# A Fourier layer with a top-k MoE on one core: the first stage as one 98 by 98 product, and DRAM scratch laid out for all partitions

## The chip, the cores and the metric

The kernel runs on one core of a Trainium2 chip. The metric is the time of one execution on the device in microseconds (us); lower is better. PE is TensorE, ACT is ScalarE, DVE is VectorE, POOL is GpSimd, SP is SyncE, which here only starts DMAs.

## The reference, cut to what matters

The input x is 8 x 3136 x 256 fp32. A real FFT over the 3136 rows of a batch, a complex 256 x 256 product with bias, a soft threshold and the inverse FFT give y. A gate then scores every row of y; the 128 best rows of each batch get the result of a two-layer network added, weighted by the sigmoid of their score.

```python
X = np.fft.rfft(x, axis=1)                     # 8 x 1569 x 256
Yr = Xr @ w_r - Xi @ w_i + b_r
Yi = Xr @ w_i + Xi @ w_r + b_i
Yr = np.sign(Yr) * np.maximum(np.abs(Yr) - 0.01, 0.0)   # Yi alike
y = np.fft.irfft(Yr + 1j * Yi, n=3136, axis=1)
scores = y @ w_gate
top_idx = np.argpartition(-scores[b], 128)[:128]        # per batch
xe = y[b, top_idx]
ye = np.maximum(xe @ w1, 0.0) @ w2
out[b, top_idx] = xe + sigmoid(scores[b, top_idx])[:, None] * ye
```

## The kernel before, in words

The 3136 rows are seen as 98 x 32, and both transforms are done in two steps by matrix products, with scratch arrays in DRAM between the steps because the steps need different axes on the partitions.

- `ld_x` loads x, one tile (`xt`) for two calls of the first step, into partitions 0..48 and 64..112: rows a and a + 49 of the 98 side by side. `fold` (L391) makes their sum and difference (`sd`), two instructions per call, on POOL; for batch 0 mostly on DVE.
- `s1` (L402) multiplies `sd` by cosines and sines: four fp32 products of 49 x 49 with 512 columns, one on each 64 x 64 quadrant of the array. ACT copies the result to `at` (L404), and a store puts it into the scratch `As`. There are 8 calls per batch.
- `ld_a` loads `av` from `As`, one tile for two groups; `s2` (L448) does the second step in 32 small fp32 products on quadrants. ACT writes the rounded half `Xh` (L454), DVE the rest `Xl` (L455). There are 13 groups per batch, 104 in all, one for each iteration of the main loop.
- `spectral` (L222 to L224) makes the complex product in 18 fp32r matmuls. ACT copies a part out (`ks`, L469), POOL adds the bias (`kb`, L471), DVE adds the two (`py`, L475). `shrink` does the threshold with ACT (`r`, L480) and DVE (`Y`, L482).
- `s2i` (L500) is the first step back; ACT copies it to `ct` (L507), DVE takes the scores on the way (`junk`, `Csc`, L509), and a store puts `ct` into the scratch `Cs`. `ld_c` loads `cv` from there, `s1i` (L547) is the last step, ACT copies to `ot` (L549), and `ov` stores go to the output.
- `route`, `select` and `place` find the best rows with many small DVE instructions (L239, L243, L265 among them) and small products on PE (L250) that share the PSUM tile `pca` with `s2i`. `fetch` and `ffn` (L325 to L372) gather them, run the network (L353 its first product) and scatter the rows.

The order is written out by hand in the loop `for t in range(-1, B * G + 20)`. An iteration flushes the stores of the one before it on SP, issues loads on SP, and then runs s2 of group t+1, one call of s1 or s1i, spectral of group t, s2i of group t-1, shrink of group t, and a second call of s1 or s1i if one is due. s1 works 17 groups ahead of s2 (`LEAD`), s1i 18 behind (`LAG`). `av` has two buffers and is asked for two iterations before its use.

DMAs are started on SP's queue or on ACT's. `move` (L151) puts the second half of x, As, av, cv and output transfers on a list, and `issue_late` (L157 to L159) issues that list on ACT's queue, in an iteration right behind the spectral product: behind `ks`, ahead of `ct`.

```python
def move(odd, out, src):
    if odd:
        late.append((out, src))
    else:
        nc.sync.dma_start(out=out, in_=src)
...
    py, r = spectral(*divmod(t, G), lambda: turn("db"))
...
issue_late()
for b, i in steady(t + LEAD + 2):
    fold(b, i, nc.gpsimd)
...
s2i(*divmod(t - 1, G))
```

Of the kernel before, what the change touches and what calls it, by code (L numbers as in the profile page):

```python
# [27 lines left out]
def _tables():  # L28
    m = np.arange(NH)
    n2 = np.arange(N2)  # L30
    n4 = np.arange(64)
    w = np.zeros((2, 64, 3, 64))
    we, wi = w[0, :NH, :2], w[0, :NH, 2]
    g = np.zeros((2, 2, N2, NJ - 1, 3, N2))
    gi = np.zeros((2, 2, N2, NP, 2, 2, 64))
    for j in range(NJ - 1):
        e = 2 * j + 2
        for p, r in enumerate((e, NH - e if e < NH else 0)):
            a = 2 * np.pi * ((m * r) % N1) / N1
# [20 lines left out]
    we[:, 0, NH - 1] = 1.0  # L60
    we[:, 1, NH - 1] = 1.0 - 2.0 * (m % 2)
    wi[NH - 1, :NH] = 1.0
    w[1] = w[0]
    gt = np.zeros((2, N2, 3, NF))
    gti = np.zeros((NF, 2, 64))
    slots = [(0, 98 * k2) for k2 in range(17)] + [(1, 49 + 98 * k2) for k2 in range(16)]
    for s, (q, k) in enumerate(slots):
        a = 2 * np.pi * ((n2 * k) % S) / S
        edge = k in (0, S // 2)
        gt[q, :, 0, s] = np.cos(a)  # L70
        gt[q, :, 1, s] = -np.sin(a)
# [8 lines left out]
    return (w.reshape(128, 3, 64), g.reshape(128, NJ - 1, 3 * N2), gi.reshape(128, NP, 2, 128),  # L80
            gt.reshape(NF, 3, NF), gti, wq.reshape(NJ, 4, N1))
# [19 lines left out]
def fourier_moe(ctx: ExitStack, tc: tile.TileContext, x, w_r, w_i, b_r, b_i, wg, w1, w2,  # L101
                t_w, t_wq, t_g, t_gi, t_gt, t_gti, t_m, t_dig, outs, cap):
# [10 lines left out]
    xv = x.rearrange("b (h m c) d -> b m h c d", h=2, c=N2)  # L113
    ov = [o.rearrange("(a r c i) d -> c a r (i d)", r=16, c=2, i=2) for o in outs]
    As, Cs, xt, sd, at, ct, av, cv, ot, X, Y, Csc = [{} for _ in range(12)]
    pca, pcb = [ps.tile([128, 2 * D], F32, name=n, bufs=1) for n in ("pca", "pcb")]

# [3 lines left out]
    w = c_tile([128, 3, 64], F32, "w")  # L121
    nc.scalar.dma_start(out=w, in_=t_w)
    xts, cvs = [[c_tile([128, 8, D], F32, n + str(k)) for k in range(2)] for n in ("xt", "cv")]
    for k, t in enumerate(xts + cvs):
        (nc.vector if k % 2 else nc.gpsimd).memset(t[32:64], 0.0)
# [251 lines left out]
    def ld_x(b, i):  # L377
        if i % 2:
            return
        k = i // 2  # L380
        t = xt[b, k] = (cvs if b == 0 and k > 1 else xts)[k % 2].rearrange("p (h c) d -> p h c d", h=2)
        for r in (1, 0):
            move(r, t[64 * r:64 * r + 48], xv[b, :48, :, 8 * k + 4 * r:8 * k + 4 * r + 4, :])
        ld(t[48:113:64], xv[b, 48, :, 8 * k:8 * k + 8, :].rearrange("h (r c) d -> r h c d", r=2))

    def fold(b, i, eng):
        e = i % 2
        t = xt[b, i // 2][:, :, 2 * e:2 * e + 2, :]
        f = sd[b, i] = pool.tile([128, 2, 2, D], F32, name="sd", bufs=2)
        for k, op in enumerate((ALU.add, ALU.subtract)):  # L390
            eng.tensor_tensor(out=f[:113, k], in0=t[:113, 0], in1=t[:113, 1], op=op)  # L391

    def s1(b, i):
        if i == 0:
            As[b] = dram.tile([2, NH, N2, D], F32, name="As")
        if i % 2 == 0:
            at[b] = pool.tile([128, 2, 2, 2 * D], F32, name="ot" if b == 0 and i > 3 else "at", bufs=2)
        f = sd.pop((b, i))
        p = ps.tile([128, 2, 2 * D], F32, name="px" if b == 0 and i % 2 else "s", bufs=1)
        for r in range(2):  # L400
            for c in range(2):
                nc.tensor.matmul(p[64 * c:64 * c + 64, r, :], w[64 * r:64 * r + NH, c, :], f[64 * r:64 * r + NH, c], start=True, stop=True)  # L402
        t = at[b]
        nc.scalar.copy(out=t[:, :, i % 2, :], in_=p)  # L404
        if i % 2 == 0:
            return

        def store():
            n = slice(4 * i - 4, 4 * i + 4)
            for q in range(2):  # L410
                move(q, As[b][q, :48, n, :], t[64 * q:64 * q + 48])
            nc.sync.dma_start(out=As[b][:, 48, n, :], in_=t[48:113:64])
# [251 lines left out]
    issue_late()  # L664
    consts_g(1)
    first = {i + 1: i for i in range(U)}
    fold(1, 0, nc.gpsimd)
    fold(1, 1, nc.gpsimd)
    rest = [(b, i) for b in range(B) for i in range(U)]
    for t in range(-1, B * G + 20):  # L670
# [3 lines left out]
        if t + 4 in first and first[t + 4] > 3:  # L674
# [41 lines left out]
        for b, i in steady(t + LEAD + 2):  # L716
            fold(b, i, nc.gpsimd)
        if t + 2 in first and first[t + 2] > 1:
            fold(1, first[t + 2], nc.gpsimd)
# [40 lines left out]
```

## Time and profile before

| what | value |
|---|---|
| three runs | 854.99, 855.54 (median), 863.56 us |
| the profiled execution | 854.73 us, its span 853.0 us |
| PE busy (matmuls) | 703.0 us, 82% of the span |
| DVE, ACT, POOL busy | 516.5, 368.8, 304.6 us |
| TensorE clock granted, mean of the span | 0.902 of full |
| DMA | 163.74 MB in 87757 packets, mean 192 GB/s |

Busy is the time in which an engine's instructions run; overlapping matmuls are counted once. [...] "DMA share" is the mean busy share of the 16 DMA engines. In a row, "x8" is a count of records (one fp32 matmul leaves two), and "[2.04 <-DVE Csc L509]" says that the engine sat idle for 2.04 us before it, until Csc was written by line 509. ACTq and SPq are the instruction queues of ACT and SP, where a DMA issue stands.

### The profile page before, as it was taken

To read this page: it belongs to the slowest core of one execution; us is meant where nothing else is said; L and a number is where in the kernel's file an instruction comes from. 1 tells how busy PE (TensorE), PEld (TensorE's weight loads), DVE (VectorE), ACT (ScalarE), POOL (GpSimd) and SP (SyncE) were. 2 spreads that over 40 slices of the span, in tenths; PEclk is the share of its full clock that TensorE was granted. 3 is DMA by queue.
4 is the path that set the end of the run, shared out by engine and by line. 5 is a ranking of instruction groups with operands and counts; after the bars stand their busy time and mean duration, and the time that the engine had idled before them with its cause. 6 is when DMAs were issued, how large, how long until landed. Compare 5 with 4: busy or idle time off the path is not lost. (4 is left out here: it accounts for less than half of the span.)

```text
span 853.0 us, 20524 instructions
## 1 busy us (share of the span) xinstructions
PE 703.0 (82%) x8220; PEld 517.0 (61%) x8220; DVE 516.5 (61%) x1339; ACT 368.8 (43%) x667; POOL 304.6 (36%) x264
## 2 busy tenths in 40 slices
PE   2749899988788978888898889888889888778876
PEld 0337667665565656565676667666667677645465
DVE  3415456544377867765457757676457989971640
ACT  1315455545354544354354434455455444532200
POOL 2126574444354524444334424346341311220000
PEclk9859999999899998898899989899899999995679
DMA  9878998999889897889798877889877748659600
GB/s 164 227 188 176 234 232 187 238 266 263 198 232 228 215 219 181 208 218 224 158 234 228 202 169 167 216 202 238 196 197 194 191 106 172 172 131 215 154 25 13
DMA packets 87757, 163.74 MB, mean 192 GB/s; under 512 B 7697, under 2 KB 61038, under 8 KB 81390
## 3 DMA queue, kind: packets, MB, share of 16 engines
q1 hardware_dynamic: 59230, 97.23, 45.6%
q10 hardware_dynamic: 27536, 63.02, 32.6%
q0 software_dynamic: 896, 2.17, 0.9%
q8 instruction: 65, 1.06, 0.6%
q14 instruction: 30, 0.25, 0.1%
HBM read 84.35 MB, written 78.12 MB: 190 GB/s over the span
## 5 line engine op out<-in xcount | busy, mean ns | idle before, releaser
L471 POOL TENSOR_TENSOR kb<-ks,bias 128x512 f32<-128x512 f32 (+1 forms) x104 | 133.9, 1287 | 414.9 <-ACT ks L469 403.1
L391 POOL TENSOR_TENSOR sd<-xt 113x512 f32<-113x512 f32 x114 | 143.4, 1279 | 33.0 <-DMA xt<-in_x 18.9
L475 DVE TENSOR_TENSOR py<-py,kb 128x512 f32<-128x512 f32 (+1 forms) x104 | 72.3, 695 | 108.1 <-POOL kb L471 79.8
L507 ACT COPY ct<-pcb 128x256 f32<-128x256 f32 x96 | 35.7, 371 | 228.8 <-PE pcb L500 173.8
L455 DVE TENSOR_TENSOR Xl<-px,Xh 128x768 fp32r<-128x768 f32 x96 | 91.9, 957 | 58.5 <-ACT Xh L454 58.2
L448 PE MATMUL px<-g_sb,av 64*64 64x96 f32 x3072 | 90.5, 250 | 35.7 <-DMA av<-As 33.6
L448 PEld LDWEIGHTS px<-g_sb,av 64*64 64x64 f32 x3072 | 81.4, 136 | 60.3 <-DMA av<-As 25.2
L500 PE MATMUL pca<-Y,gi_sb 64*64 64x256 f32 x768 | 108.6, 403 | 0.0
L500 PE MATMUL pcb<-Y,gi_sb 64*64 64x256 f32 x768 | 108.5, 403 | 0.0
L454 ACT CAST Xh<-px 128x768 fp32r<-128x768 f32 x96 | 77.2, 805 | 41.7 <-PE px L448 23.5
L402 PE MATMUL s<-sd,w 49*64 49x512 f32 x480 | 74.1, 646 | 20.3 <-DVE sd L391 15.4
L547 PE MATMUL s<-cv,w 49*64 49x512 f32 x464 | 73.6, 660 | 17.2 <-ACT ot L549 16.8
L480 ACT ACTIVATE r<-py,m2l 128x512 f32<-128x512 f32 (+1 forms) x104 | 72.4, 696 | 31.6 <-DVE py L475 31.4
L509 DVE CUSTOM_DVE_ANT_0 junk<-pcb,wgb 128x256 f32<-128x256 f32 x96 | 40.4, 421 | 62.5 <-ACT ct L507 61.7
L222 PE MATMUL pcb<-wsh,Xh 128*128 128x256 f32 x208 | 72.6, 349 | 1.5 <-DVE Csc L509 1.5
L482 DVE SCALAR_TENSOR_TENSOR Y<-py,r 128x512 f32<-128x512 f32 (+1 forms) x104 | 71.2, 685 | 2.9 <-ACT r L480 2.9
L222 PEld LDWEIGHTS pcb<-wsh,Xh 128*128 128x128 f32 x208 | 42.7, 205 | 45.9 <-issue 28.3
L404 ACT COPY at<-s 128x1024 f32<-128x1024 f32 x58 | 59.9, 1033 | 21.9 <-PE s L402 21.4
L549 ACT COPY ot<-s 128x1024 f32<-128x1024 f32 x58 | 59.2, 1021 | 19.6 <-PE s L547 18.0
L500 PEld LDWEIGHTS pca<-Y,gi_sb 64*64 64x64 f32 x768 | 47.5, 139 | 29.3 <-issue 6.1
L222 PE MATMUL py<-wnh,Xh 128*128 128x256 f32 x208 | 62.8, 302 | 1.3 <-DVE Y L482 1.2
L222 PE MATMUL py<-wdh,Xh 128*128 128x256 f32 x208 | 62.9, 303 | 0.0
(133 smaller groups left out, 1503.6 us busy)
## 6 DMA issues: line engine op xcount, KB each, us to landing
Cs<-ct SPq DMA_DIRECT2D x48, 512.0 KB
av<-As ACTq DMA_DIRECT2D x48, 256.0 KB
av<-As SPq DMA_DIRECT2D x48, 256.0 KB
xt<-in_x ACTq DMA_DIRECT2D x30, 384.0 KB
xt<-in_x SPq DMA_DIRECT2D x30, 384.0 KB
As<-at ACTq DMA_DIRECT2D x30, 384.0 KB
As<-at SPq DMA_DIRECT2D x30, 384.0 KB
cv<-Cs SPq DMA_DIRECT2D x30, 384.0 KB
```

Source lines behind the costliest of these rows:

```text
L222: nc.tensor.matmul(out, wh, mh, start=start, stop=False)
L391: eng.tensor_tensor(out=f[:113, k], in0=t[:113, 0], in1=t[:113, 1], op=op)
L402: nc.tensor.matmul(p[64 * c:64 * c + 64, r, :], w[64 * r:64 * r + NH, c, :], f[64 * r:64 * r + NH, c], start=True, stop=True)
L448: nc.tensor.matmul(o[:, :, N2 * j:N2 * j + N2], a[64 * p:64 * p + 64, 2 * (g % 2) + j, 128 * h + 64 * q:128 * h + 64 * q + 64], g_sb[64 * ...
L454: nc.scalar.copy(out=vh, in_=v)
L455: nc.vector.tensor_tensor(out=vl, in0=v, in1=vh.bitcast(F32), op=ALU.subtract)
L471: nc.gpsimd.tensor_tensor(out=kb[:r], in0=ks[:r].broadcast_to([r, 2, D]), in1=bias[:r], op=ALU.add)
L475: nc.vector.tensor_tensor(out=py[:r], in0=py[:r], in1=kb[:r], op=ALU.add)
L480: nc.scalar.activation(out=r1[:r], in_=py[:r], func=AF.Relu, bias=m2l[:r], scale=1.0)
L482: nc.vector.scalar_tensor_tensor(out=y[:r], in0=py[:r], scalar=0.0, in1=r1[:r], op0=ALU.min, op1=ALU.add)
L500: nc.tensor.matmul(p[q][64 * a:64 * a + 64], gi_sb[64 * q:64 * q + 64, g, c, 64 * a:64 * a + 64], y[64 * q:64 * q + 64, c, :], start=(c == ...
L547: nc.tensor.matmul(p[64 * c:64 * c + 64, r, :], w[64 * r:64 * r + NH, 2, :], f[64 * r:64 * r + NH, 4 * e + 2 * c:4 * e + 2 * c + 2, :], st ...
```

## The change

The first step is one 98 x 98 product per 512 columns, on x as it lies in DRAM. `fold` and its tiles are gone. `xt` holds one of the 98 rows on each of 98 partitions, and there are three such buffers instead of two. `As` is 98 x 32 x 256. `Cs` is 2 x 64 x 32 x 256 in three fixed DRAM tiles with 15 rows of padding per half, which `pads` fills with zeros once, at t = 3. `Cs` stores come in two, one for even and one for odd rows; `cv` loads span 128 partitions. Output runs are 4 KB. Columns of `gi` and `gti` are permuted to match. `warm`, which runs matmuls on constants, stands at the very start and gets a POOL memset and four DVE transposes. At the start, batch 1 gets three x tiles ahead instead of two, and every second s1 copy of batch 0 is on DVE. x, As, av and cv are no longer split over `move`.

```diff
     def ld_x(b, i):
-        t = xt[b, k] = (cvs if b == 0 and k > 1 else xts)[k % 2].rearrange("p (h c) d -> p h c d", h=2)
-        for r in (1, 0):
-            move(r, t[64 * r:64 * r + 48], xv[b, :48, :, 8 * k + 4 * r:8 * k + 4 * r + 4, :])
-        ld(t[48:113:64], xv[b, 48, :, 8 * k:8 * k + 8, :].rearrange("h (r c) d -> r h c d", r=2))
+        t = xt[b, k] = (xts[:2] + cvs)[k] if b == 0 else xts[(4 * b + k + 1) % 3]
+        ld(t[:96], xv[b, :96, 8 * k:8 * k + 8, :])
+        ld(t[96:N1], xv[b, 96:, 8 * k:8 * k + 8, :])
-    def fold(b, i, eng):
-        e = i % 2
-        t = xt[b, i // 2][:, :, 2 * e:2 * e + 2, :]
-        f = sd[b, i] = pool.tile([128, 2, 2, D], F32, name="sd", bufs=2)
-        for k, op in enumerate((ALU.add, ALU.subtract)):
-            eng.tensor_tensor(out=f[:113, k], in0=t[:113, 0], in1=t[:113, 1], op=op)
     def s1(b, i):
-        for r in range(2):
-            for c in range(2):
-                nc.tensor.matmul(p[64 * c:64 * c + 64, r, :], w[64 * r:64 * r + NH, c, :], f[64 * r:64 * r + NH, c], start=True, stop=True)
+        for h in range(2):
+            n = 4 * (i % 2) + 2 * h
+            nc.tensor.matmul(p[:N1, h, :], w, f[:N1, n:n + 2, :], start=True, stop=True)
-        nc.scalar.copy(out=t[:, :, i % 2, :], in_=p)
+        if b == 0 and i % 2:
+            nc.vector.tensor_copy(t[:N1, i % 2], p[:N1])
+        else:
+            nc.scalar.copy(out=t[:N1, i % 2], in_=p[:N1])
...
-            for q in range(2):
-                move(q, As[b][q, :48, n, :], t[64 * q:64 * q + 48])
-            nc.sync.dma_start(out=As[b][:, 48, n, :], in_=t[48:113:64])
+            nc.sync.dma_start(out=As[b][:96, n, :], in_=t[:96])
+            nc.sync.dma_start(out=As[b][96:, n, :], in_=t[96:N1])
     def ld_a(b, g):
...
-            for q in range(2):
-                move(q, av[b, g][64 * q:64 * q + 64], As[b][q, :48].rearrange("(j c) n d -> (c n) j d", c=2)[:, 2 * g:2 * g + 4])
+            ld(av[b, g], As[b][:96].rearrange("(j c) n d -> (c n) j d", c=4)[:, 2 * g:2 * g + 4])
     def s2i(b, g):
...
-            stores.append(lambda: nc.sync.dma_start(out=Cs[b][:48].rearrange("(j q) n d -> (q n) j d", q=2)[:, 2 * g - 2:2 * g + 2], in_=t))
+            def store():
+                for q in range(2):
+                    nc.sync.dma_start(out=Cs[b][q, :48].rearrange("(j a) n d -> (a n) j d", a=2)[:, 2 * g - 2:2 * g + 2], in_=t[q::2])
+            stores.append(store)
+    def pads():
+        z = pool.tile([128, 2, 2, 2 * D], F32, name="ot", bufs=2).rearrange("p r s (o x) -> p o (r s x)", o=1)
+        nc.gpsimd.memset(z, 0.0)
+        for t in Csd:
+            for q in range(2):
+                ld(t[q, NH:].rearrange("m n d -> m (n d)").rearrange("m (k x) -> m k x", k=4), z[:64 - NH].broadcast_to([64 - NH, 4, 2048]))
     def ld_c(b, i):
-        for r in range(2):
-            move(r, t[64 * r:64 * r + 48], Cs[b][:48, 16 * k + 8 * r:16 * k + 8 * r + 8, :])
-        ld(t[48:113:64], Cs[b][48, 16 * k:16 * k + 16].rearrange("(r n) d -> r n d", r=2))
+        ld(t, Cs[b].rearrange("r m n d -> (r m) n d")[:, 8 * k:8 * k + 8, :])
     def s1i(b, i):
...
             for c in range(2):
-                move(c, ov[b][c, :48, n, :], t[64 * c:64 * c + 48].rearrange("p r s x -> p (r s) x"))
+                move(c, ov[b][c, :48, i // 2], t[64 * c:64 * c + 48].rearrange("p r s x -> p r (s x)"))
...
+    warm()
     for i in range(U):
         ld_x(0, i)
-    issue_late()
...
         if i == 4:
             ld_x(1, 0)
             ld_x(1, 2)
+            ld_x(1, 4)
         flush()
-        issue_late()
     weights()
-    warm()
```

On ACT, in iteration t = 40 (batch 3, group 1), the order of before is this; `DMA` rows are issues on ACT's queue, the rest are its own copies.

```order
L469 COPY ks<-pcb 128x256
L159 DMA As<-at 48x2048
L159 DMA out<-ot 48x4x512
L159 DMA xt_73<-in_x 48x2x1024
L159 DMA av<-As 64x4x256
L507 COPY ct<-pcb 128x256
L507 COPY ct<-pca 128x256
L480 ACTIVATE r_3593<-py,m2l 128x512
L454 CAST Xh<-px 128x2x12x32
L404 COPY at<-s 128x2x512
```

The changed kernel has this there.

```order
L467 COPY ks<-pcb 128x256
L165 DMA out<-ot 96x1x1024
L505 COPY ct<-pcb 128x256
L505 COPY ct<-pca 128x256
L478 ACTIVATE r_3365<-py,m2l 128x512
L452 CAST Xh<-px 128x2x12x32
L405 COPY at<-s 98x1024
```

Three of the four DMA issues between `ks` and `ct` have left ACT; only the half of the output store is still there.

On SP, in the iterations t = 40 to t = 42 (there is nothing for it to issue in t = 41), from the output store on, before has this; every row is a DMA issue.

```order
L155 DMA out<-ot 48x4x512
L557 DMA out<-ot 2x4x512
L155 DMA xt_73<-in_x 48x2x1024
L149 DMA xt_73<-in_x 2x2x1024
L155 DMA av<-As 64x4x256
L515 DMA Cs<-ct 128x4x256
L155 DMA av<-As 64x4x256
L155 DMA cv_74<-Cs 48x2048
L149 DMA cv_74<-Cs 2x2048
```

The changed kernel:

```order
L161 DMA out<-ot 96x1x1024
L565 DMA out<-ot 2x2x1024
L155 DMA xt_78<-in_x 96x2048
L155 DMA xt_78<-in_x 2x2048
L155 DMA av<-As 128x4x256
L518 DMA Cs_72<-ct 64x4x256 x2
L155 DMA av<-As 128x4x256
L155 DMA cv_80<-Cs_71 128x2048
```

What was split over both queues stands whole on SP's, in the same order; the `av` load behind a `Cs` store is now the whole tile, not half of it.

## Rows read from the trace of the kernel before

**Rows 1.** windows by stage: us, busy us (xrecords), PEclk, DMA share, GB/s
```profile
0.00:52.00 52.00, 21.53 (x78) 8.78 (x78) 17.95 (x25) 9.90 (x10) 13.64 (x14) 0.86 0.83 192
52.00:660.00 608.00, 527.67 (x6688) 393.02 (x6692) 374.49 (x908) 295.95 (x540) 258.66 (x220) 0.92 0.87 211
660.00:767.00 107.00, 88.33 (x1153) 70.23 (x1142) 95.53 (x274) 47.35 (x96) 25.37 (x23) 0.97 0.65 156
```

**Rows 2.** waits of PE, 52 to 660 us: us in total, times, longest
```profile
PE px L448 <- DMA av<-As: 33.6, 19, 10.2
PE s L547 <- ACT ot L549: 16.8, 8, 3.4
PE pca L250 <- DVE Csc L509: 15.8, 8, 2.7
```

**Rows 3.** timeline of ACT around iteration t = 40: start, us, instruction
```profile
311.28 0.37 ACT L469 COPY ks<-pcb 128x256 f32<-128x256 f32 x1 [0.29 <-PE pcb L224]
...
312.20 2.27 ACTq L159 DMA_DIRECT2D xt<-in_x  x1
314.51 2.28 ACTq L159 DMA_DIRECT2D av<-As  x1
316.89 0.37 ACT L507 COPY ct<-pcb 128x256 f32<-128x256 f32 x1 [5.24 <-DMA out<-ot]
```

**Rows 4.** timeline of PE, two stretches
```profile
315.30 1.03 PE L402 MATMUL s<-sd,w 49*64 49x512 f32 x8
318.36 0.17 PE L250 MATMUL pca<-n,tm 98*98 98x6 bf16 x1 [2.04 <-DVE Csc L509]
...
333.38 0.17 PE L250 MATMUL pca<-n,tm 98*98 98x6 bf16 x1 [2.67 <-DVE Csc L509]
```

**Rows 5.** ACT's av issues by source line L159: ns min/median/max, first and last start
```profile
L159 ACTq DMA_DIRECT2D av<-As x48: 580/592/2737, 43.1 to 728.4; - x48
```

**Rows 6.** timeline of POOL, 325 to 334 us
```profile
327.49 1.27 POOL L471 TENSOR_TENSOR kb<-ks,bias 128x512 f32<-128x512 f32 x1 [3.00 <-ACT ks L469]
328.73 2.49 POOL L391 TENSOR_TENSOR sd<-xt 113x512 f32<-113x512 f32 x2
```

**Rows 7.** timeline of DVE, 328 to 337 us, the same instruction twice
```profile
330.06 1.38 DVE L243 TENSOR_TENSOR c<-scores,f 98x192 bf16<-98x192 f32 x1
...
336.69 0.36 DVE L243 TENSOR_TENSOR c<-scores,f 98x192 bf16<-98x192 f32 x1
```

**Rows 8.** windows of POOL, L391 (the folds) alone, 52 to 660 us
```profile
52.00:660.00 608.00, 136.02 (x108) 0.92 0.87 211
```

**Rows 9.** windows, two short stretches, all engines
```profile
324.10:334.20 10.10, 7.41 (x127) 5.46 (x120) 9.04 (x19) 5.44 (x11) 4.12 (x4) 1.00 0.91 212
334.40:337.60 3.20, 3.20 (x20) 2.74 (x23) 3.03 (x8) 0.68 (x2) 1.28 (x1) 0.50 0.86 182
```

**Rows 10.** windows at the start, columns as in rows 1
```profile
4.00:9.00 5.00, 0.00 (x0) 0.00 (x0) 1.14 (x1) 0.38 (x1) 0.29 (x1) 1.00 1.02 156
9.00:15.00 6.00, 0.00 (x0) 0.00 (x0) 0.32 (x1) 0.00 (x0) 0.00 (x0) 1.00 1.04 218
...
50.00:52.00 2.00, 0.00 (x0) 0.00 (x0) 0.00 (x0) 0.00 (x0) 0.00 (x0) 0.50 1.01 267
```

**Rows 11.** timeline of DVE at the first fold
```profile
14.68 1.90 DVE L391 TENSOR_TENSOR sd<-xt 113x512 f32<-113x512 f32 x3 [9.54 <-DMA xt<-in_x]
```

**Rows 12.** timeline of PE at the first s2
```profile
52.23 1.56 PE L448 MATMUL px<-g_sb,av 64*64 64x96 f32 x32 [10.16 <-DMA av<-As]
```

**Rows 13.** windows of PE, L402 (s1) alone, 52 to 660 us
```profile
52.00:660.00 608.00, 63.08 (x448) 15.60 (x448) 0.92 0.87 211
```

**Rows 14.** records of s1 by source line: ns min/median/max, first and last start
```profile
L402 PE MATMUL s<-sd,w x480: 587/591/1113, 15.4 to 641.8; 49*64 49x512 f32 x160
```

**Rows 15.** timeline of PE at the FFN's first product, full array, fp32
```profile
838.82 2.05 PE L353 MATMUL m<-xT,w1s 128*128 128x128 f32 x16 [0.52 <-DVE xT L338]
```

**Rows 16.** waits of SP's queue, 52 to 660 us
```profile
SPq L515 <- ACT ct L507: 108.0, 31, 8.6
```

More of the change, by code (lines that the diff above doesn't have):

```diff
@@ L31, in _tables @@
     n4 = np.arange(64)
-    w = np.zeros((2, 64, 3, 64))
-    we, wi = w[0, :NH, :2], w[0, :NH, 2]
+    n1 = np.arange(N1)
+    o4 = 2 * (n4 % 32) + n4 // 32
+    wf = np.zeros((N1, NJ - 1, 2, 2))
+    wl = np.zeros((N1, 2))
+    wi = np.zeros((64, 64))
     g = np.zeros((2, 2, N2, NJ - 1, 3, N2))
@@ L72, in _tables @@
         a = 2 * np.pi * ((n4 * k) % S) / S
-        gti[s, 0] = (1.0 if edge else 2.0) * np.cos(a) / S
-        gti[s, 1] = (0.0 if edge else -2.0) * np.sin(a) / S
+        gti[s, 0, o4] = (1.0 if edge else 2.0) * np.cos(a) / S
+        gti[s, 1, o4] = (0.0 if edge else -2.0) * np.sin(a) / S
     gt[:, :, 2] = gt[:, :, 0] + gt[:, :, 1]
@@ L111, in fourier_moe @@
     dram = ctx.enter_context(tc.tile_pool(name="scratch", bufs=3, space=bass.MemoryType.DRAM))
-    xv = x.rearrange("b (h m c) d -> b m h c d", h=2, c=N2)
-    ov = [o.rearrange("(a r c i) d -> c a r (i d)", r=16, c=2, i=2) for o in outs]
-    As, Cs, xt, sd, at, ct, av, cv, ot, X, Y, Csc = [{} for _ in range(12)]
+    xv = x.rearrange("b (a c) d -> b a c d", c=N2)
+    ov = [o.rearrange("(a r k c e i) d -> c a k r (e i d)", r=2, k=4, c=2, e=2, i=2) for o in outs]
+    As, Cs, xt, at, ct, av, cv, ot, X, Y, Csc = [{} for _ in range(11)]
     pca, pcb = [ps.tile([128, 2 * D], F32, name=n, bufs=1) for n in ("pca", "pcb")]
+    Csd = [dram.tile([2, 64, N2, D], F32, name="Cs" + str(k), bufs=1) for k in range(3)]
     def c_tile(shape, dt, name):
         return const.tile(shape, dt, name=name)
-    w = c_tile([128, 3, 64], F32, "w")
+    w = c_tile([N1, N1], F32, "w")
     nc.scalar.dma_start(out=w, in_=t_w)
-    xts, cvs = [[c_tile([128, 8, D], F32, n + str(k)) for k in range(2)] for n in ("xt", "cv")]
-    for k, t in enumerate(xts + cvs):
-        (nc.vector if k % 2 else nc.gpsimd).memset(t[32:64], 0.0)
+    wi_sb = c_tile([128, NF], F32, "wi_sb")
+    nc.scalar.dma_start(out=wi_sb, in_=t_wi)
+    xts = [c_tile([128, 8, D], F32, "xt" + str(k)) for k in range(3)]
+    cvs = [c_tile([128, 8, D], F32, "cv" + str(k)) for k in range(2)]
     g_sb = c_tile([128, NJ - 1, 3 * N2], F32, "g_sb")
@@ L417, in ld_a @@
             av[b, g] = pool.tile([64, 1, D], F32, name="av", bufs=2)
-            for q in range(2):
-                ld(av[b, g][N2 * q:N2 * q + N2, 0, :], As[b][q, 48])
+            ld(av[b, g][:, 0, :], As[b][96:].rearrange("c n d -> (c n) d"))
         elif g % 2 == 0:
             av[b, g] = av[b, g + 1] = pool.tile([128, 4, D], F32, name="av", bufs=2)
-            for q in range(2):
-                move(q, av[b, g][64 * q:64 * q + 64], As[b][q, :48].rearrange("(j c) n d -> (c n) j d", c=2)[:, 2 * g:2 * g + 4])
+            ld(av[b, g], As[b][:96].rearrange("(j c) n d -> (c n) j d", c=4)[:, 2 * g:2 * g + 4])
     def s2(b, g):
@@ L487, in s2i @@
         if g == 0:
-            Cs[b] = dram.tile([NH, 64, D], F32, name="Cs")
+            Cs[b] = Csd[b % 3]
             Csc[b] = pool.tile([128, NJ], F32, name="Csc")
@@ L512, in s2i, with store @@
         if w == 1:
-            stores.append(lambda: nc.sync.dma_start(out=Cs[b][48], in_=t[:r, o, :]))
+            def store():
+                for q in range(2):
+                    nc.sync.dma_start(out=Cs[b][q, 48], in_=t[q:64:2, o, :])
+            stores.append(store)
         elif g % 2 == 1:
-            stores.append(lambda: nc.sync.dma_start(out=Cs[b][:48].rearrange("(j q) n d -> (q n) j d", q=2)[:, 2 * g - 2:2 * g + 2], in_=t))
+            def store():
+                for q in range(2):
+                    nc.sync.dma_start(out=Cs[b][q, :48].rearrange("(j a) n d -> (a n) j d", a=2)[:, 2 * g - 2:2 * g + 2], in_=t[q::2])
+            stores.append(store)
     def score(b):
@@ L525, in score @@
         for q in range(4):
-            nc.tensor.matmul(p, wq[:, q, :], t[:, N2 * q:N2 * q + N2], start=(q == 0), stop=(q == 3))
+            nc.tensor.matmul(p, wq[:, q, :], t[:, 64 * (q // 2) + q % 2:64 * (q // 2) + 64:2], start=(q == 0), stop=(q == 3))
         yield "da"
         nc.vector.tensor_copy(scores[:, b, :], p)
+    def pads():
+        z = pool.tile([128, 2, 2, 2 * D], F32, name="ot", bufs=2).rearrange("p r s (o x) -> p o (r s x)", o=1)
+        nc.gpsimd.memset(z, 0.0)
+        for t in Csd:
+            for q in range(2):
+                ld(t[q, NH:].rearrange("m n d -> m (n d)").rearrange("m (k x) -> m k x", k=4), z[:64 - NH].broadcast_to([64 - NH, 4, 2048]))
     def ld_c(b, i):
@@ L546, in s1i @@
             for c in range(2):
-                nc.tensor.matmul(p[64 * c:64 * c + 64, r, :], w[64 * r:64 * r + NH, 2, :], f[64 * r:64 * r + NH, 4 * e + 2 * c:4 * e + 2 * c + 2, :], start=True, stop=True)
+                nc.tensor.matmul(p[64 * c:64 * c + 64, r, :], wi_sb[64 * r:64 * r + NH], f[64 * r:64 * r + NH, 4 * c + 2 * e:4 * c + 2 * e + 2, :], start=True, stop=True)
         t = ot[b]
@@ L567, in warm @@
             nc.tensor.matmul(p[:, i % 2], pr[:, :128], pr[:, :512], start=True, stop=True)
+        a = pool.tile([128, 2, 2, 2 * D], F32, name="ot", bufs=2).rearrange("p a b c -> p (a b c)")
+        nc.gpsimd.memset(a, 0.0)
+        v = a.rearrange("p (n d) -> p d n", d=64)[:, :16]
+        nc.vector.transpose(out=v, in_=v)
+        nc.vector.transpose(out=a[:, :512], in_=a[:, :512])
+        nc.vector.transpose(out=v, in_=p[:, 0].rearrange("p (n d) -> p d n", d=16))
+        nc.vector.transpose(out=a[:, :512], in_=p[:, 1])
     YB, XB, KB, RB = 2, 2, 1, 1
@@ L653, in fourier_moe @@
     for i in range(U):
-        fold(0, i, nc.gpsimd if i % 3 == 2 else nc.vector)
         s1(0, i)
@@ L673, in fourier_moe @@
             ld_x(b, i)
-        if t + 4 in first and first[t + 4] > 3:
+        if t + 4 in first and first[t + 4] > 5:
             ld_x(1, first[t + 4])
@@ L689, in fourier_moe @@
             consts_gi((t + 1) // 2 + 1)
+        if t == 3:
+            pads()
         if t == 8:
@@ L715, in fourier_moe @@
         issue_late()
[L716 to L719, printed above, removed]
         tick(ffns)
```

38 lines of the change are left out of this document (17 added, 21 removed).

## The prediction

> **What bounds the kernel now.** I read the windows by stage first: before the first s2 (0 to 52 us), the main stretch up to the last s1 (52 to 660), the rest of the main loop without x and s1 (660 to 767). What lies behind 767 is routing, FFN and last stores, which the change does not touch. In the main stretch PE is busy 527.7 of 608 us; DVE has 374, ACT 296, POOL 259 [rows 1]. So PE bounds it, with 80.3 us of gaps, and a mean granted clock of 0.92, which costs (1 - 0.92) x 608 = 49 us. Together 129 us lie beside PE's work at full clock. From 660 to 767 DVE is busy 95.5 of 107 us and bounds; no edit takes anything from DVE's work there, so this stretch and the tail count as 0.
>
> Next, who ends PE's gaps. The list of waits names av loads first (33.6 us, of which 10.2 is the one at the start), then copies of ACT and the scores of DVE [rows 2]. An engine in such a list is only the last link, so I went back along two gaps.
>
> The first: PE waits 2.04 us at 318.36 for `Csc`, DVE's reading of what s2i left [rows 4]. DVE reads it behind `ct`, and `ct` starts late: on ACT, between `ks` at 311.28 and `ct` at 316.89, stand DMA issues, two of 2.3 us each, and ACT does nothing else in that time [rows 3]. An av issue on ACT takes 0.59 us in the median but up to 2.7 [rows 5].
>
> The second: PE waits 2.67 us at 333.38, again for `Csc` [rows 4]. Here DVE itself is late. Its instruction of L243 takes 1.38 us while POOL runs `kb` and two folds (327.49 to 331.2), and 0.36 us at 336.69 with POOL's folds out of the way [rows 6, 7]. Folds are 136 of POOL's 259 us [rows 8, 1]; `kb` stays.
>
> [...]
>
> **The change, part by part.**
>
> *The s1 product (cost).* A call is now eight records on quadrants, four at a time: one of 0.59 us [rows 14], all in 1.03 us [rows 4], so the second round starts 0.44 us behind the first. Two full-array fp32 products leave four records, one behind the other: 0.59 + 3 x 0.44 = 1.91 us, 0.88 more. A check from the full array: 16 records of 128 columns take 2.05 us [rows 15], as many columns as four of 512, so 0.8 to 1.0 more. Between 52 and 660 us lie 448 / 8 = 56 calls [rows 13]: **+49 us** (45 to 57), all on the bounding engine. The eight calls of the start wait for x and cost nothing.
>
> *The start (gain).* Up to 9 us only one half of x comes, into 48 partitions: all DMA engines are busy (1.02) but move 156 GB/s; with both halves 218, with loads over 128 partitions 267 [rows 10]. The first fold waits 9.54 us for x, the first s2 10.16 us for av, at 52.23 [rows 11, 12]. By then 52 x 192 GB/s = 10.0 MB have moved [rows 1]; the third x tile of batch 1 adds 98 x 8 KB = 0.8 MB. 10.8 MB at 267 GB/s take 40 us: **-12 us**. At 218 it is 49.5 (-3); without the third tile in the way 37.5 (-15).
>
> [...] The rows of 218 and 267 GB/s, which differ with both halves in flight, are why I stay with 12.
>
> *Gaps of PE (gain).* av: 33.6 - 10.2 = 23.4 us. What makes these loads late is ACT's queue (their second half stands behind `ks` and other issues) and slow x loads ahead of them in the same engines; both go, and I take 18 of 23.4. The other 80.3 - 23.4 = 57 us come from folds, from ACT's issues and from causes that stay (`kb`, output issues, dependences). I take the folds' share of POOL's time, 136 / 259 = 0.53: 30. Together **-48 us**. Bounds: a third of everything, or 85 in 100.
>
> *Clock (gain).* If 48 of 80.3 us of gaps go, 0.6 of the 49 us goes too: **-29 us**.
>
> *Padding, longer loads.* `pads` writes 6 x 15 rows of 32 KB = 2.95 MB, 14 us of DMA time at 211 GB/s, once, beside a loop in which DMA is busy 0.87 [rows 1]: between 0 and 14 us, I take **+2**, since PE has two av buffers to live on. The 128-partition cv loads read 128 instead of 98 rows, 32 x 30 x 8 KB = 8 MB in all, 29 us of DMA time at 267 GB/s. Against it, x's 25.7 MB at 267 instead of about 187 (midway of 156 and 218) save 41 us of it: 0. If that cover fails, it shows as av waits, priced below.
>
> *SP's queue (a risk).* Issues that left ACT stand in SP's queue, which is in order. There a `Cs` store waits for `ct`, 108 us in 31 waits, up to 8.6 each [rows 16], and the av issue stands behind it; before, ACT's half of av went around it. av is asked for two iterations ahead (608 us for 88 iterations, 6.9 each, so 13.8), a mean wait is 3.5: I take 0.
>
> *At nothing:* three x buffers, odd copies of batch 0 on DVE, `warm` and its transposes (DVE and PE are idle up to the first x), 4 KB output runs, permuted tables.
>
> **Sum**, against the profiled execution (854.73; it stands 0.8 under the median, which I leave out): 854.7 - 12 + 49 - 48 - 29 + 2 = **817 us**. A measurement tells 1% from no change: 847 to 864 is "the same".
>
> **The rivals.**
>
> *Nearly all gaps go.* For it: both gaps followed back lead to things that are removed. Against: `kb` stays, routing still waits on DVE. 85 in 100 of 129 is 110, the start -15: 854.7 - 15 + 49 - 110 + 2 = 781 us.
>
> *x loads don't get faster:* not the partitions but the short runs and their distance in DRAM make 156 GB/s. For it: runs are 4 KB now, and no load of x into 98 partitions stands in the trace. Against: one half alone is slower than both. Then the start gains 3, av 8, the other gaps 30, the clock 38 / 80.3 x 49 = 23: 854.7 - 3 + 49 - 38 - 23 + 2 = 842 us.
>
> *Dependences keep the gaps.* Only a third of the 129 us (43) comes back, because PE, ACT and DVE wait for each other in a ring once the issues are gone: 854.7 - 12 + 49 - 43 + 2 = 851 us, no change to tell. For it: ACT's copies and `Csc` are the last links in rows 2.
>
> *SP becomes the bound of av (slower).* Its place is the av issue behind a `Cs` store. If av comes 1 us too late for each of the 44 pairs of iterations of the main stretch, 44 us of gaps arise and 0.6 x 44 = 27 of half clock: 817 + 44 + 27 = 888 us. It is slower than before from (855 - 817) / (1.6 x 44) = 0.54 us per pair on. For it: the 8.6 us wait. Against: 3.5 in the mean of 13.8.
>
> **How the numbers follow.** Forecast 817: 0.52. Nearly all gaps 781: 0.16. x loads as slow 842: 0.11. A third 851: 0.09. SP 888: 0.12. Faster by over 1%: 0.52 + 0.16 + 0.11 = 0.79; same 0.09; slower 0.12. The range leaves out the SP case (0.12) and half of the 781 case (0.08), and takes in 851: 776 to 852 us.
>
> **What would show it.** In the profile after: the first s2 near 40 us, DMA above 218 GB/s while x comes; s1's records near 0.5 us, four in 1.9, PE busier by 49 us in the main stretch less what the clock gives back; no folds, DVE's L243 at 0.36 except beside `kb`; `ct` less than 1 us behind the end of s2i; PE's waits for av under 10 us; PEclk near 0.97 in the main stretch. It is wrong if PE's gaps stay at 60 us or more there, if av leads the waits again, or if the first s2 stays near 50 us.

## The result, and the profile after

The changed kernel takes 827.6 us (median; 824.05 to 832.16) against 855.6: a ratio of 0.9655, 95% interval 0.9576 to 0.9734. Faster by 3 to 4%, inside the range, 11 us above the forecast of 817. The profiled execution is the slowest of the four, 832.16 us, span 830.4.

The windows by stage of the changed kernel: before the first s2, up to the last s1, the rest of the loop (columns as in rows 1).

```profile
0.00:43.00 43.00, 19.30 (x46) 9.09 (x46) 13.88 (x19) 5.95 (x6) 2.01 (x5) 0.83 0.87 247
43.00:623.00 580.00, 523.27 (x6288) 379.70 (x6291) 329.40 (x883) 291.65 (x528) 124.05 (x111) 0.96 0.78 230
623.00:727.00 104.00, 89.93 (x1198) 73.67 (x1194) 92.52 (x247) 46.49 (x92) 24.21 (x21) 0.96 0.55 171
```

Against [rows 1] the start is 9 us shorter, and POOL has lost half its work. The middle rows do not hold the same work: the one of before runs 18 us past the last s1 record, this one 4. Cut at the first s2 and at the last s1, before and then after, they are these.

```profile
52.23:641.80 589.57, 509.50 (x6472) 378.76 (x6472) 360.00 (x875) 286.88 (x524) 254.83 (x217) 0.91 0.88 212
43.23:618.80 575.57, 519.07 (x6249) 376.01 (x6249) 327.26 (x878) 289.77 (x525) 122.77 (x110) 0.96 0.78 230
```

So the main stretch is 14 us shorter, and PE's gaps (span less PE busy) went from 80.1 to 56.5 us. The list of PE's waits, over the whole span, does not look repaired:

```profile
PE px L446 <- DMA av<-As: 41.6, 9, 25.8
PE px L446 <- issue: 19.8, 1, 19.8
PE pca L256 <- DVE Csc L507: 9.5, 8, 1.7
PE s L556 <- ACT ot L558: 6.9, 11, 0.7
```

The waits for Csc and ot have shrunk [rows 2], while av is worse, for one wait of 25.8 us. It is in PE's timeline here:

```profile
112.41 1.56 PE L446 MATMUL px<-g_sb,av 64*64 64x96 f32 x32 [25.75 <-DMA av<-As]
```

And this is what SP's queue did ahead of it:

```profile
67.08 0.39 SPq L155 DMA_DIRECT2D av<-As  x1
67.52 0.50 SPq L155 DMA_DIRECT2D gi_sb<-t_gi  x1
68.12 19.53 SPq L155 DMA_DIRECT2D Cs<-ot  x6
87.70 4.89 SPq L155 DMA_DIRECT2D g_sb<-t_g  x1
92.70 4.56 SPq L411 DMA_DIRECT2D As<-at  x1
97.30 3.12 SPq L412 DMA_DIRECT2D As<-at  x1
100.52 3.08 SPq L518 DMA_DIRECT2D Cs<-ct  x2
103.69 0.96 SPq L155 DMA_DIRECT2D xt<-in_x  x2
104.69 0.39 SPq L155 DMA_DIRECT2D av<-As  x1
```

`Cs<-ot` x6 are the zero blocks. Their issue takes 19.53 us, the three behind them 3 to 5 each, and the next av is asked for 37.6 us after the last. The windows of that time show what the DMA engines did meanwhile:

```profile
60.00:75.00 15.00, 15.00 (x176) 11.18 (x178) 7.47 (x17) 7.92 (x15) 5.58 (x4) 1.00 0.80 228
75.00:86.00 11.00, 11.00 (x140) 8.04 (x136) 5.99 (x14) 6.52 (x12) 2.19 (x2) 1.00 0.93 111
86.00:100.00 14.00, 0.66 (x15) 0.15 (x4) 2.16 (x6) 1.23 (x3) 0.37 (x1) 0.64 0.85 107
100.00:113.00 13.00, 0.59 (x16) 0.62 (x20) 0.00 (x0) 0.00 (x0) 0.00 (x0) 0.50 0.91 283
```

From 75 to 100 us the DMA engines are 0.85 to 0.93 busy and move only 107 to 111 GB/s, while the zeros leave the 15 partitions that hold them. Without the blocks the DMA engines, as busy (0.94), move 276 GB/s in the stretch that has 111 here (e1, below).

The start: x now comes into 96 partitions at 236 to 246 GB/s [rows 10].

```profile
2.00:6.00 4.00, 2.13 (x5) 1.75 (x6) 1.92 (x2) 1.81 (x2) 0.55 (x1) 1.00 0.98 243
6.00:9.00 3.00, 3.00 (x10) 2.32 (x10) 0.00 (x0) 0.00 (x0) 0.00 (x0) 1.00 1.02 246
9.00:14.00 5.00, 4.73 (x12) 1.72 (x11) 2.59 (x3) 1.01 (x1) 0.00 (x0) 1.00 1.03 236
```

What comes late there is av. On SP's queue its issue follows the last store of batch 0 into As by 10 us:

```profile
29.47 0.23 SPq L412 DMA_DIRECT2D As<-ot  x1
39.29 0.38 SPq L155 DMA_DIRECT2D av<-As  x1
```

On ACT, iteration t = 40 [rows 3] now has one issue, and `ct` waits for PE, not for ACT:

```profile
318.05 0.37 ACT L467 COPY ks<-pcb 128x256 f32<-128x256 f32 x1
318.13 0.58 ACTq L165 DMA_DIRECT2D out<-ot  x1
320.47 0.37 ACT L505 COPY ct<-pcb 128x256 f32<-128x256 f32 x1 [2.05 <-PE pcb L498]
```

An s1 call leaves four records in 1.96 us instead of eight in 1.03 [rows 4]:

```profile
321.00 1.96 PE L400 MATMUL s<-xt,w 98*98 98x512 f32 x4
```

To compare the same work, the next rows run from the `ks` copy of group 12 to that of group 80. First before, then after:

```profile
129.30:609.20 479.90, 412.42 (x5150) 305.39 (x5149) 303.45 (x743) 232.61 (x423) 197.65 (x165) 0.91 0.88 213
```

The changed kernel, the same groups:

```profile
147.60:582.80 435.20, 410.20 (x4982) 295.67 (x4981) 272.05 (x746) 233.94 (x423) 96.00 (x83) 1.00 0.80 244
```

Span less PE busy are gaps: 67.5 and 25.0 us. (1 - PEclk) x span is what half clock costs: 43 and about 0. PE's own work, busy less half clock, has grown from 369 to 410. So the loop won 44.7 us there. By the start of `ks`, in order: up to group 6 the kernel gained 13 us, groups 6 to 8 lost 30 (98.0 to 108.7 before, 84.6 to 125.6 after), 8 to 80 gained 43, the rest lost 4 (from 80 to the end of the span 243.8 before, 247.6 after). These 4 us lie ahead of the last s1 record (32.6 us before, 36.0 after), where three longer s1 calls stand; behind it both take 211 us.

### The profile page after: what moved, and what is told of

It reads as the page before. It is cut to its first block, busy times and chain, and to the rows that moved or that the text cites. A ratio compares the mean times of both kernels' runs of the same rounds, so it can differ in the third digit from the quotient of the medians.

```text
span 830.4 us, 19603 instructions
## 1 busy us (share of the span) xinstructions
PE 711.4 (86%) x7964; PEld 516.1 (62%) x7964; DVE 478.4 (58%) x1333; ACT 366.7 (44%) x663; POOL 161.1 (19%) x148
## 3 DMA queue, kind: packets, MB, share of 16 engines
q8 instruction: 63, 1.03, 0.5%
## 5 line engine op out<-in xcount | busy, mean ns | idle before, releaser
L446 PE MATMUL px<-g_sb,av 64*64 64x96 f32 x3072 | 85.9, 248 | 63.3 <-DMA av<-As 41.6
L400 PE MATMUL s<-xt,w 98*98 98x512 f32 x232 | 116.4, 625 | 4.3 <-ACT ot L558 4.3
L498 PE MATMUL pca<-Y,gi_sb 64*64 64x256 f32 x768 | 104.4, 391 | 0.0
L498 PE MATMUL pcb<-Y,gi_sb 64*64 64x256 f32 x768 | 104.4, 391 | 0.0
L405 ACT COPY at<-s 98x1024 f32<-98x1024 f32 x58 | 58.9, 1015 | 48.3 <-PE s L400 34.0
L228 PE MATMUL pcb<-wsh,Xh 128*128 128x256 f32 x208 | 76.1, 366 | 0.6 <-DVE Csc L507 0.6
L556 PE MATMUL s<-cv,wi_sb 49*64 49x512 f32 x464 | 68.6, 622 | 6.9 <-ACT ot L558 6.9
L400 PEld LDWEIGHTS s<-xt,w 98*98 98x98 f32 x232 | 34.2, 166 | 43.6 <-issue 32.2
L230 PE MATMUL pcb<-wsl,Xh 128*128 128x256 f32 x208 | 59.7, 287 | 0.0
L229 PE MATMUL pcb<-wsh,Xl 128*128 128x256 f32 x208 | 59.7, 287 | 0.0
```

The costliest lines, as they stand in the source:

```text
L228: nc.tensor.matmul(out, wh, mh, start=start, stop=False)
L229: nc.tensor.matmul(out, wl, mh, start=False, stop=False)
L400: nc.tensor.matmul(p[:N1, h, :], w, f[:N1, n:n + 2, :], start=True, stop=True)
L446: nc.tensor.matmul(o[:, :, N2 * j:N2 * j + N2], a[64 * p:64 * p + 64, 2 * (g % 2) + j, 128 * h + 64 * q:128 * h + 64 * q + 64], g_sb[64 * ...
L498: nc.tensor.matmul(p[q][64 * a:64 * a + 64], gi_sb[64 * q:64 * q + 64, g, c, 64 * a:64 * a + 64], y[64 * q:64 * q + 64, c, :], start=(c == ...
L556: nc.tensor.matmul(p[64 * c:64 * c + 64, r, :], wi_sb[64 * r:64 * r + NH], f[64 * r:64 * r + NH, 4 * c + 2 * e:4 * c + 2 * e + 2, :], star ...
```

## The experiments

Ratios are to the kernel before on the same chip; differences of ratios are told as us of 855.6. "e1" and so on are the experiments in order. A ratio's interval is 5 to 9 us to either side, and the difference of two is less certain still; where intervals overlap it is said.

**e1: no zero blocks.**

```diff
-        if t == 3:
-            pads()
-        ld(t, Cs[b].rearrange("r m n d -> (r m) n d")[:, 8 * k:8 * k + 8, :])
+        for r in range(2):
+            ld(t[64 * r:64 * r + NH], Cs[b][r, :NH, 8 * k:8 * k + 8, :])
```

> The changed kernel without the zero blocks: pads is gone, and cv is loaded by two DMAs of 49 partitions, so that the padding rows are never touched. Theory (the zero blocks hold up SP's queue, av comes 25.75 us late, and half clock follows): 25.75 us of gap and some 4 us of half clock go, 827.6 - 30 = 798 us (794 to 803), no gap over 5 us of PE between 50 and 115 us. Rival (av is late there for the DMA traffic of the start, and the wait comes back at the next av): 818 us or more, with av waits of 15 us or more between 50 and 150 us.

Measured 802.3 us, 0.9396 (0.9318 to 0.9474): 22 us below the changed kernel by ratios, 25 by medians. In the stretch of the gap PE now runs through and the DMAs bring 276 GB/s:

```profile
75.00:86.00 11.00, 11.00 (x140) 8.06 (x136) 6.13 (x14) 6.52 (x12) 2.00 (x3) 1.00 0.94 276
86.00:100.00 14.00, 14.00 (x191) 10.04 (x192) 7.83 (x20) 7.96 (x16) 4.83 (x9) 1.00 0.94 272
```

The theory holds; its 30 us were somewhat too many.

**e2: the same six blocks, one in every second iteration** (`pads(n)` issues the n-th).

```diff
-        if t == 3:
-            pads()
+        if t in range(3, 15, 2):
+            pads((t - 3) // 2)
```

> The changed kernel with the same six zero blocks, one at a time at t = 3, 5, ... 13 instead of six at t = 3. Theory (what costs is that six issues stand one behind the other ahead of As stores and av loads on one queue): each holds SP for at most 19.5 / 6 = 3.3 us, av has 13 us of lead, and the time is that without the blocks plus 0 to 6: 798 to 806 us. Rival (the bytes cost: 2.95 MB at 107 to 111 GB/s are 27 us in which the DMA engines bring nothing else): 815 us or more.

804.0 us, 0.9409 (0.9338 to 0.9479), not to be told from e1. One at a time, the issue of a block takes 0.93 us, not 19.53 / 6 = 3.3:

```profile
L155 SPq DMA_DIRECT2D Cs<-ot x6: 896/927/1013, 66.3 to 125.3; - x6
```

The bytes cost nothing that can be told, and neither do the 128-partition cv loads, which e1 took out as well and e2 keeps. Six blocks in a row, issued on SP's queue ahead of As and av, cost the 22 us.

**e3: no zero blocks, x of batch 1 later.**

```diff
-        if i == 4:
-            ld_x(1, 0)
-            ld_x(1, 2)
-            ld_x(1, 4)
...
     ld_a(0, 0)
+    ld_x(1, 0)
+    ld_x(1, 2)
+    ld_x(1, 4)
```

> As the kernel without zero blocks, with the three x tiles of batch 1 asked for behind the first av load instead of ahead of the last As stores of batch 0. Theory (2.4 MB of x stand ahead of the last As stores in the DMA engines, and the first s2 waits for them): 2.4 MB at 236 GB/s are 10 us, the first s2 comes at about 34 instead of 43 us, and the time is 8 to 10 us below that without zero blocks: 789 us. Rival (the first s2 waits for a chain of latencies, store, landing, load, and x only comes later): within 3 us of the kernel without zero blocks.

800.6 us, 0.9352 (0.9255 to 0.9449), not to be told from e1: the time is the rival's, not the theory's 789. The first s2 comes earlier, as in the theory (33.8 against 43.5 us), but the second av, now behind that x, gives it back: at group 4 the lead is down from 10 us to 3.

**e4: the kernel before, all DMAs on SP.**

```diff
-        if odd:
-            late.append((out, src))
-        else:
-            nc.sync.dma_start(out=out, in_=src)
+        nc.sync.dma_start(out=out, in_=src)
```

> The kernel before with one part of the change alone: every DMA that move gave to ACT's queue is issued on SP's. Theory (ACT's issues ahead of ct are a main cause of PE's gaps, the folds the other): of the 129 us of gaps and half clock 15 to 25 go, 830 to 840 us, PE's waits for ot and Csc fall by half. First rival (the folds are the cause, ACT's issues were hidden): 851 to 858 us. Second rival (SP's queue becomes the bound, av behind Cs stores): 868 us or more, av leads PE's waits with 60 us or more.

815.0 us, 0.9550 (0.9480 to 0.9621): one part of the change, with nothing else of it, takes 38 us, more than the theory's 15 to 25 and at least as much as the whole change (the two intervals overlap). Groups 12 to 80:

```profile
118.60:573.80 455.20, 396.17 (x5150) 295.14 (x5149) 307.96 (x743) 232.54 (x423) 197.79 (x165) 0.94 0.92 224
```

Half clock falls from 43 to 27 us, the gaps only from 67.5 to 59.0. Of the 43.1 us between the two profiled executions 24.7 lie in these groups, 10.7 ahead of them and 7.6 behind. The theory's sign hardly came: summed over all rows of a wait, PE waited 27.2 us for Csc in these groups and now 17.9, for ot 21.0 and now 22.3. Its waits for av went from 18.1 to 10.5 us, those for cv from 0.3 to 7.6. The largest rows before, beside the one for Csc in [rows 2]:

```profile
PE px L448 <- DMA av<-As: 18.1, 13, 3.3
PE s L547 <- ACT ot L549: 16.1, 7, 3.4
```

With all DMAs on SP:

```profile
PE s L544 <- ACT ot L546: 16.8, 7, 3.5
PE pca L247 <- DVE Csc L506: 14.9, 10, 2.7
PE px L445 <- DMA av<-As: 10.5, 13, 1.8
PE s L544 <- DMA cv<-Cs: 7.6, 4, 3.0
```

So what ACT's issues cost is shown, but the waits expected for it went only in small part: 40 us for ot and Csc are left of 48. SP's queue, with everything on it, did not become the bound.

**e5: e1 with POOL's two instructions per s1 call back** (`fold` as before, on halves of one x tile).

```diff
+        for b, i in steady(t + LEAD + 2):
+            fold(b, i, nc.gpsimd)
```

> The changed kernel without zero blocks (802 us), with two POOL instructions per s1 call put back where the folds stood in the iteration, on x, into a tile that nothing reads. Theory (the folds on POOL, which stretch DVE's instructions, are what keeps 59 us of PE's gaps in the kernel before when all DMAs are on SP, against 25 in the changed kernel): most of the 34 us of gaps and 21 of half clock between t = 12 and t = 80, scaled to the whole loop (about 1.2), come back: 840 to 865 us, PE's waits for Csc and ot lead. Rival (those gaps come from the slow x loads and the busier DMA engines of the old layout; POOL is idle beside them): 812 us or less.

812.2 us, 0.9514 (0.9410 to 0.9618): 10 us above e1, with overlapping intervals. The theory fell, and the rival's bound of 812 us is where the time lies; beside the 98 by 98 product a cost of the folds is not shown. Nothing waits for these two instructions, here and in e10, so a wait of s1 for its fold is not in their price.

**e6: e1 with s1 on quadrants**, for batches 1 to 7.

```diff
-        for h in range(2):
-            nc.tensor.matmul(p[:N1, h, :], w, f[:N1, n:n + 2, :], start=True, stop=True)
+        for r in range(2):
+            for c in range(2):
+                nc.tensor.matmul(p[64 * c:64 * c + 64, r, :], wi_sb[64 * r:64 * r + 34], f[64 * r:64 * r + 34, n:n + 2, :], start=True, stop=True)
```

> The changed kernel without zero blocks, where s1 of batches 1 to 7 is four products on quadrants again, taken on 2 x 34 rows of x as they are; the rest of the sum is left out, there are no folds. PE has 0.86 us less in each of 56 calls, 48 in all. Theory (the main stretch is bound by PE, 419 of 442 us busy): 38 to 48 us go, 754 to 764 us. Rival (with PE shorter, the ring of ACT, DVE and POOL behind spectral, or av, sets the time): 780 us or more, with PE's gaps longer by 25 us or more.

783.9 us, 0.9170 (0.9067 to 0.9273): 19 us less, not 48. The rival is nearer.

**e7: e1 with the halves on ACT again** (shown for av; x, As and cv alike).

```diff
-            ld(av[b, g], As[b][:96].rearrange("(j c) n d -> (c n) j d", c=4)[:, 2 * g:2 * g + 4])
+            for q in range(2):
+                move(q and (b > 0 or g > 2), av[b, g][64 * q:64 * q + 64], As[b][:96].rearrange("(j q c) n d -> q (c n) j d", q=2, c=2)[q, :, 2 * g:2 * g + 4])
```

> The changed kernel without zero blocks, with half of every x and As transfer from batch 2 on, of av (from group 4 of batch 0 on) and of cv issued by move on ACT's queue again, behind ks and ahead of ct; the layout stays. Theory (ACT's issues ahead of ct delay ct, Csc and ot, wherever the data lie: the kernel before lost 45 us to them): 835 to 850 us. Rival (they cost because x loads into 48 partitions were slow and held DMA queue places; with the new layout they are hidden): 812 us or less.

861.5 us, 1.0092 (1.0039 to 1.0145): 60 us above e1, 1% above the kernel before, and beyond the theory's 850. New layout, one product and no folds bring nothing while these issues stand on ACT. The transfers are cut into halves again, too; e4 issues such halves on SP and gains, which speaks against the cutting as the cause. The av issues there behave as in [rows 5]:

```profile
L165 ACTq DMA_DIRECT2D av<-As x46: 581/596/2825, 59.5 to 730.4; - x46
```

PE's largest wait in groups 12 to 80 is again for av, first in e1, then in e7; waits for Csc come to 11 us more, those for ot to no more than in e1.

```profile
PE px L446 <- DMA av<-As: 8.1, 5, 2.3
PE px L449 <- DMA av<-As: 25.1, 14, 7.8
```

**e8: e3 with the output halves on SP too** (the edit of e4 on top of e3).

> No zero blocks, x of batch 1 behind the first av (800.6 us), and the last DMA issues that are still on ACT in the loop, 32 halves of output stores, on SP too. Theory (each of them costs 0.3 to 2 us ahead of ct): 5 to 12 us less, 789 to 796 us. Rival (32 of them are hidden, as ct waits for PE there): within 3 us of 800.6. Slower than 805 if SP's queue, now with all issues, holds av back.

786.1 us, 0.9215 (0.9116 to 0.9313): 12 us below e3 by ratios, though the intervals overlap, for 32 issues of 0.58 us, 18.7 us in all. It is also 38 us below the changed kernel. Groups 12 to 80:

```profile
116.00:547.50 431.50, 413.18 (x4982) 297.59 (x4982) 272.16 (x746) 233.41 (x424) 95.83 (x83) 0.99 0.79 236
```

**e9: e8 with s1 on quadrants** (the edit of e6).

> The kernel with all DMAs on SP, no zero blocks and x of batch 1 later (786 us), with s1 of batches 1 to 7 on quadrants, on 2 x 34 rows of x as they are (the rest of the sum is left out, no folds): 48 us less for PE. Theory (PE is paced by a ring of engines in part of the iterations, so that only part of s1's extra work is paid, as 18 us were with 32 issues left on ACT): 762 to 774 us. Rival (with no issue left on ACT the main stretch is bound by PE in full): 738 to 748 us.

768.3 us, 0.8980 (0.8925 to 0.9034): 20 us below e8. Groups 12 to 80:

```profile
107.70:527.20 419.50, 389.46 (x5150) 286.98 (x5149) 284.07 (x743) 230.93 (x424) 95.76 (x83) 0.97 0.80 244
```

PE is busy 24 us less than in e8, about 32 less without half clock, but its gaps grow from 18.3 to 30.0 and half clock from 4 to 13. The span falls by 12: nearly two thirds of what s1 costs had been filling time in which PE would have waited or run at half clock.

**e10: e9 with POOL's folds** (the edit of e5).

> As the one with s1 on quadrants and all DMAs on SP, with two POOL instructions per s1 call put back where the folds stood. It has the engines' work of the kernel before with all DMAs on SP (815 us) in the new layout. Theory (folds cost more where PE has less to do: they are what held that one): 20 us or more above the kernel without folds. Rival (folds cost 10 us here as they did beside the 98 by 98 product, and the layout of x, As, Cs and out makes the rest): 7 to 13 us above it, 775 to 785 us.

802.7 us, 0.9388 (0.9333 to 0.9443): 35 us above e9. Groups 12 to 80, gaps 51.5 and half clock 27 us:

```profile
107.40:558.70 451.30, 399.81 (x5150) 296.98 (x5150) 309.63 (x743) 231.23 (x423) 197.33 (x165) 0.94 0.75 225
```

DVE does the same work in 26 us more (309.6 against 284.1). One instruction of select shows it, in the groups by line (count | busy us, mean ns | idle before); first e9, then e10:

```profile
L246 DVE TENSOR_TENSOR c<-scores,f 98x192 bf16<-98x192 f32 x30 | 13.8, 459 | 0.9
```

With folds:

```profile
L246 DVE TENSOR_TENSOR c<-scores,f 98x192 bf16<-98x192 f32 x30 | 26.2, 873 | 0.9
```

It was 864 ns in the kernel before and is 486 in the changed one. POOL's work is the only edit between 459 and 873 ns, so it is what lengthens the instruction; by what means is not shown. With POOL's work PE's waits for ot and Csc come back, most of which e4 had left (107 to 559 us; e9, then e10):

```profile
PE s L558 <- ACT ot L560: 9.3, 10, 1.5
PE pca L253 <- DVE Csc L508: 6.2, 10, 1.1
```

With folds:

```profile
PE s L565 <- ACT ot L567: 18.8, 9, 3.5
PE pca L253 <- DVE Csc L515: 15.4, 9, 2.7
```

**e11: the kernel before, ACT's issues behind `r`.**

```diff
-        issue_late()
...
             shrink(*divmod(t, G), py, r)
+        issue_late()
         pair()
```

> The kernel before, with its DMA issues still on ACT's queue but placed behind shrink's r instead of ahead of ct. Theory (their place ahead of ct is what costs, because ct, Csc and the PSUM tiles behind them are what PE waits for): 815 to 832 us, nearly as with all on SP (815). Rival (an issue on ACT costs wherever it stands, since ks, ct, r, Xh and ot fill every iteration in order): 845 to 858 us.

935.7 us, 1.0951 (1.0881 to 1.1020): far beyond both expectations. ACT's timeline:

```profile
407.94 2.51 ACTq L159 DMA_DIRECT2D av<-As  x1
410.49 0.80 ACT L454 CAST Xh<-px 128x768 fp32r<-128x768 f32 x1 [2.26 <-PE pcb L224]
```

The issue now stands ahead of `Xh` and `ot`, and half of av is asked for later. PE's waits over the span, 33.6 and 16.8 us before:

```profile
PE px L448 <- DMA av<-As: 66.5, 23, 7.4
PE s L547 <- ACT ot L549: 34.3, 11, 6.4
```

Neither of the two places tried in ACT's order was free; the one before was the better.

**e12: e8 with x of batch 1 behind the second av.**

```diff
     ld_a(0, 0)
-    ld_x(1, 0)
-    ld_x(1, 2)
-    ld_x(1, 4)
...
             ld_a(*divmod(t + 3, G))
+        if t == -1:
+            for i in (0, 2, 4):
+                ld_x(1, i)
```

> As the one with all DMAs on SP (786 us), with the three x tiles of batch 1 behind the second av load. Theory (the second av waits 4.3 us behind 2.4 MB of x, and half clock follows): 4 to 7 us less, 779 to 782 us. Rival (x of batch 1 is then late for its s1, and the gain is gone by t = 8): within 3 us of 786.

782.0 us, 0.9154 (0.9094 to 0.9214): the fastest kernel that computes everything, as the theory had it, but not to be told from e8.

## Why the prediction was right, and where its terms were not

The time lay in the range by luck as much as by its terms: s1 cost 29 us less than forecast, the zero blocks 20 more. A path from before to after, by ratios: all DMAs on SP -38 us (e4); new layout, start and 4 KB runs, with nearly the same work for PE and POOL, -14 (e4 to e10); folds off -35 (e10 to e9); s1 as one product +20 (e9 to e8); 32 output issues back on ACT, x of batch 1 earlier again +15 (e8 to e1); six zero blocks in a row +22 (e1 to after). Together -30. The steps may depend on their order, as e5 suggests for the folds, and the -14 is what remains between two kernels, not an edit of its own.

Of the prediction's three signs of being wrong, one came: av leads the waits again (41.6 us), through one wait of 25.8 us. The gaps stayed just under its 60 us (56.5), and the first s2 came at 43. That its main stretch was cut 18 us behind the last s1 changes nothing: up to there the gaps are 80.1 us.

- *s1's product.* The size was right: 0.88 us was forecast, 1.96 - 1.03 = 0.93 stands in the two rows. That it is "all on the bounding engine" was the step that failed: its 49 us cost 20 (e8, e9) and 19 (e1, e6). PE was busy 82% of the span, but when its work was taken away its gaps grew (18.3 to 30.0 us in e9): in part of the iterations others set the pace.
- *Padding*, +2: failed, 22. Bytes were weighed, and "beside a loop" taken for cover. What counted was six blocks in a row on the queue that As and av stand on: one at a time they cost nothing that can be told (e2). That few partitions made them slow is the author's estimate, from 111 GB/s against the 276 of e1; no run varied their number. The prediction did name where it would show, as av waits. That "PE has two av buffers to live on" does not help when the next av is issued 37.6 us after the last.
- *The start*, -12: -9. x loads came at 236 to 246 GB/s, not at 267, but the rival of loads that stay slow has fallen. PE then sat idle for 19.8 us ahead of the first s2: SP issued av 10 us after the last As store. Part of that lay behind x of batch 1, as e3 shows.
- *Gaps*, -48, or 60 in 100: -24 from the first s2 to the last s1, where the wait at the zero blocks is new; 63 in 100 (67.5 to 25.0 us) in the groups 12 to 80, away from it. Right in size there. But the split was not: av gave 7.5 us of the 18 taken (15.9 us of waits stay behind 125 us), and the waits for Csc and ot gave 37 (48 to 11) where 30 were taken for all the rest. The first gap followed back led to ACT's issues, but with those gone 40 of the 48 us stayed (e4); POOL's folds, to which the second gap led and by which the sum sized this term, doubled such waits where they were put in, from 21 to 43 us (e9, e10). One gap followed back does not stand for the list.
- *Clock*: forecast 0.6 of it, nearly all came back (43 to 0 us in those groups). That half clock falls in proportion to gaps was the author's estimate, with the one gap of [rows 9] for it (0.50 behind it, 1.00 ahead), and no run shows it: after has 25 us of gaps and a clock of 1.00 there, before 67.5 and 0.91. From the first s2 to the last s1, with the zero blocks in it, the clock is 0.96.
- *SP's queue*, the slower rival: it did become the place of the one large wait, but through the zero blocks. Its steady form, av behind Cs stores, did not come: e4 and e8 have all issues on SP and are faster.

Open: why the folds cost 35 us beside the quadrants and 10, if anything, beside the large product (with issues left on ACT); and by what path ACT's issues cost their time. In e7 PE waits longer for av, half of which is asked for on ACT's queue (17 us), and for Csc (11), but no run moves av alone.

## What to carry to other kernels

DMA issues on an engine that copies out of PSUM can be dear though that engine is busy only 43% of the time, as ACT was here (38 us less without them in e4, 60 more with them back in e7): try them on a queue whose engine computes nothing, and look at the engine's own queue rows, not at its busy share. A one-time DMA is priced by what stands behind it on its queue (six zero blocks cost 22 us in a row, nothing to be told when spread); spread it. Work added to PE need not cost its full time where PE has gaps (s1's 49 us cost 20); price it by running the kernel with it taken away. And look whether the waits that a theory names really go: e4 gained more time than forecast, but most of those waits stayed (40 of 48 us).

## What was not expected of the hardware

With 158 issues on ACT instead of 32 the kernel took 60 us more (e7 against e1); without the 32, which take 18.7 us, 12 less (e8, intervals overlap); and issues moved by three instructions cost 82 us (e11). An issue of av took 0.58 us or 2.8 on the same line (e7); what makes some of them long was not tried. While zeros were written from 15 partitions, the DMA engines were 0.93 busy for 11 us and moved 111 GB/s.
